# Turning the last product: w_down and W' as weights, h and o as the moving operand

## The chip, the cores and the metric

The kernel runs on one core of one Trainium2 chip. The metric is the device time of one execution in microseconds (us), the median of several runs. Engines: TensorE (PE, with its weight loads as PEld), VectorE (DVE), ScalarE (ACT), GpSimd (POOL) and SyncE (SP). SP computes nothing; its queue issues most of the DMAs, one after the other in program order.

## The reference

With S = 2048 tokens, D = 512, 32 heads of 16, F = 1792, all in float32:

```
g   = sigmoid((x * gate_w).sum(-1))                       one number per token
q, k, v = heads of x @ wqkv;  phi(t) = where(t > 0, t + 1, exp(t)) + 1e-6
kv  = sum_s phi(k)_s v_s^T;   z = sum_s phi(k)_s           per head
o   = phi(q) @ kv / (phi(q) . z + 1e-6)
h   = (x @ w_gate) * (x @ w_up)
out = g * (o @ wo) + (1 - g) * (h @ w_down)                [2048, 512]
```

## The kernel before

**Precision.** Every float32 operand of the large products is split into a high and a low part in a form that TensorE multiplies at full rate. `mm3` (it calls `mm`, line 52) makes each product of three matmuls: high by high, high by low, low by high. `split` (line 66) makes the parts: ACT copies the high one (`act`, line 58), DVE subtracts (`tt`, line 61). `stt` (line 64) is DVE's operation with a scalar and two tensors.

**Stage 1** (`p1`, to about 92 us). It goes through x in 16 tiles of 128 tokens, makes k, phi(k), the matrix G = phi(k)^T x (four PSUM banks `gt`), z, and on DVE the gate sum of every token as a column of `scol` [128, 16] (line 262). After the loop come the z store (`zpark`), and four small operations that turn `scol` into `gcol` = g and `ocol` = 1 - g, one column for each block of 128 tokens (lines 348 to 351).

**Stage 2** (`p2`, the rest). Two *pairs* of chunks of 512 tokens, and for each pair 16 *units*: 14 slices of 128 columns of w_gate and w_up (`f`) and two (`q`), after slices 5 and 9, of q. A unit (`unit`) computes a 2x2 block product with seven products instead of eight (Strassen's scheme in a form with sums of x blocks and of weight blocks), in four PSUM banks Y, X, R and S of one buffer each. Banks R and S are seeded by DVE (`bR<-bX,m`, `bS<-t,bX`) before PE accumulates on them, and DVE's `t<-bR,cross` reads R between PE's product 1 and product 6 into R. For an `f` unit the result is h for two chunks (`hh`, `hl`: [128 features, 2 chunks, 512 tokens]).

The order of the work is written out by hand: all operations of PE, ACT, DVE and SP's DMAs keep program order (`keep_in_program_order`). `later(n, place, fn)` puts work into unit n at a named place, `do(n, place)` runs it; the places of a unit come in the order high, low, e, m, c, d, t, s, r, end. `w_load(n+3)` follows unit n.

**The last product.** `wp_unit` folds kv and wo into W' (four row blocks, parked in DRAM), so that o @ wo becomes (phi(q) / den) @ W'. Two units' h with two row blocks of w_down (`dh`, `dl`, split by `down_weights` from the load `wdr`, first thing at place e), or o of a `q` unit with two row blocks of W', form a *group*. `down_jobs` makes a list of 8 jobs of it, one for every block of 128 tokens of the pair. A job is six matmuls of 512 columns into a PSUM bank `pdn` (tags dn and att, two buffers each), with the h or o slice as weights and w_down or W' moving; then the bank, scaled by g or 1 - g of its tokens (a column, one number per partition), is added to the block's accumulator `acc` [128 tokens, 512] in SBUF (ACT for the first group, else DVE, line 64). With the ninth group (`ends`) the block is complete and goes out: by POOL's queue for pair 0, by SP's for pair 1 (line 595). The very last job is cut into two halves of 256 columns. `share(n)` says how many jobs run at four points of unit n; what is left runs after the last unit.

**The denominators.** `attention` sends phi(q) z terms through DRAM, adds them (`z_add`, `z_end`), takes the reciprocal (`recip`, tile [128, 128]), stores it, and loads it back broadcast over the 16 columns of a head; `norm_high` multiplies phi(q) by it.

`bmask` is a [128, 128] mask for the heads that is last read in unit 2 (`kv_split`). Tag `cb` has three buffers of [128, 512], used to prepare x sums for pair 1 until unit 13.

Of the kernel before, what the change touches and what calls it, by code (L numbers as in the profile page):

```python
# [7 lines left out]
F32 = mybir.dt.float32  # L8
F32R = mybir.dt.float32r
AF = mybir.ActivationFunctionType  # L10
# [15 lines left out]
NPAIR = NC // 2  # L26
TPP = 2 * CH // P
EPS = 1e-6
WARM = 8
LEAD = 4  # L30
HB = 8
# [12 lines left out]
def gated_mix(ctx: ExitStack, tc, xt, xp, x, wqkv, wq, wq_add, wo, wgu, wgu_add, wdn, gate_w, out):  # L44
# [12 lines left out]
    def act(dst, src, func=AF.Copy, **kw):  # L57
        pin(nc.scalar.activation(dst, src, func, **kw))  # L58
# [4 lines left out]
    def stt(dst, a, scalar, b, op0, op1):  # L63
        pin(nc.vector.scalar_tensor_tensor(dst, a, scalar, b, op0=op0, op1=op1))  # L64
# [9 lines left out]
    def mm3(dst, lhs, rhs, start, stop, on=False, late=0, part=range(3)):  # L74

        (lh, ll), (rh, rl) = lhs, rhs
        three = ((lh, rh), (ll, rh), (lh, rl)) if late else ((lh, rh), (lh, rl), (ll, rh))
        for i in part:
            mm(dst, *three[i], start=start and i == 0, stop=stop and i == 2, skip_group_check=on)
# [9 lines left out]

    epsc = const.tile([P, 1], F32, name="epsc")  # L90
    scol = const.tile([P, 2 * NT + 8], F32, name="scol")[:, 0:NT]
    gcol = const.tile([P, NT], F32, name="gcol")
    ocol = const.tile([P, NT], F32, name="ocol")
    zcol = const.tile([P, KT], F32, name="zcol")
    ezcol = const.tile([P, KT], F32, name="ezcol")
    bmask = const.tile([P, P], F32, name="bmask")
# [20 lines left out]
    xpark = {i: [dram.tile([P, 2, CH], F32, name=f"xpark{i}{v}") for v in "hl"] for i in (2, 3, 4)}  # L117
    xsum = {i: dram.tile([P, 2, CH], F32, name=f"xsum{i}") for i in (1, 5, 6, 7)}

    zpark = dram.tile([KT * KT, P, P // KT], F32, name="zpark")  # L120
    wpark = [[dram.tile([P, D], F32, name=f"wpark{b}{v}") for v in "hl"] for b in range(KT)]

# [58 lines left out]
    with tc.tile_pool(name="p1", bufs=2, reuse_waits="tile") as p1:  # L181
# [163 lines left out]
        dma(zpark.rearrange("c l e -> l c e"), zacc.rearrange("l (c e) -> l c e", e=P // KT))  # L345


        act(gcol, scol, AF.Exp, scale=-1.0)
        pin(nc.vector.tensor_scalar_add(gcol, gcol, 1.0))
        pin(nc.vector.reciprocal(gcol, gcol))  # L350
        pin(nc.vector.tensor_scalar(ocol, gcol, -1.0, 1.0, op0=ALU.mult, op1=ALU.add))


    p2 = ctx.enter_context(tc.tile_pool(name="p2", bufs=1, reuse_waits="tile"))
# [203 lines left out]
            dma(there, part.bitcast(F32))  # L558


    acc = {}

    parts = [(1, 0), (0, 1), (1, 1), (0, 0)]
    banks = ["dn", "dn"]
    left = {(p, i): NF // 2 + 1 for p in range(NPAIR) for i in range(TPP)}

    def down_jobs(pair, group, col):

        def job(i):
            t = pair * TPP + i  # L570
            c, sl = divmod(i, CH // P)
            sl = slice(sl * P, (sl + 1) * P)
            s = col[:, t:t + 1]
            first = (pair, i) not in acc
            if first:
                acc[pair, i] = p2.tile([P, D], F32, tag="acc", name="acc", bufs=8)
            else:
                left[pair, i] -= 1
            ends = not left[pair, i]

            step = D // 2 if ends and pair and i == TPP // 2 - 1 else D
            for o in range(0, D, step):
                cols = slice(o, o + step)
                banks.reverse()
                pd = psum.tile([P, D], F32, tag=banks[0], name="pdn", bufs=2)[:, 0:step]
                for j, ((hh, hl), w2) in enumerate(group() if callable(group) else group):
                    mm3(pd, (hh[:, c, sl], hl[:, c, sl]), [v[:, cols] for v in w2], j == 0, j == 1)
                a = acc[pair, i][:, cols]
                if first:
                    act(a, pd, scale=s)  # L590
                else:
                    stt(a, pd, s, a, ALU.mult, ALU.add)
                if ends:
                    to = nc.gpsimd if pair == 0 else nc.sync
                    tc.keep_in_program_order(to.dma_start(out[t * P:(t + 1) * P, cols], a))

        return [lambda i=i: job((i + TPP // 2) % TPP) for i in range(TPP)]


    def attention(pair, j, n):  # L600
        phs, group, wrow = {}, {}, {}
        den = {}
        turns = n + 5 == units

        terms = dram.tile([KT, 4 * HB, DH, P], F32, name=f"terms{pair}{j}")
        there = dram.tile([4 * HB, KT, P], F32, name=f"den{pair}{j}")

        def quad(r, c, q):

            ex = p2.tile([P, CH], F32, tag="z", name="ex", bufs=4)  # L610
            act(ex, q, AF.Exp)
            ph = phs[r, c] = p2.tile([P, CH], F32, tag="ph", name="phq", bufs=4)
            act(ph, q, AF.Relu)
            stt(ph, ex, 1.0, ph, ALU.min, ALU.add)

        def z_part(i):
            r, c = parts[i]
            b = 2 * j + r
            z = p2.tile([P, CH], F32, tag="z", name="zq", bufs=4)
            act(z, phs[r, c], AF.Identity, scale=zcol[:, b:b + 1], bias=ezcol[:, b:b + 1])  # L620
            dma(terms[:, HB * i:HB * (i + 1)].rearrange("c h e t -> (h e) c t"), z.rearrange("p (c t) -> p c t", c=KT))

        def z_load(e):

            den[e] = p2.tile([P, KT, P], F32, tag="z", name="zt", bufs=4)
            dma(den[e], terms[:, :, e * KT:(e + 1) * KT].rearrange("c h e t -> (c h) e t"))

        def z_add(e):
            tt(den[0], den[0], den[e], ALU.add)

        def z_end():
            z = den[0]
            tt(z[:, 0:2], z[:, 0:2], z[:, 2:4], ALU.add)
            den["d"] = p2.tile([P, P], F32, tag="den", name="den")
            stt(den["d"], z[:, 0], EPS, z[:, 1], ALU.add, ALU.add)

        def recip():
            d = den["d"]
            pin(nc.vector.reciprocal(d, d))
            dma(there.rearrange("h c t -> c h t"), d)  # L640

        def norm(i):
            r, c = parts[i]
            if r not in group:
                group[r] = hidden()
            rb = p2.tile([P, CH], F32, tag="z", name="rb", bufs=4)
            one = there[HB * i:HB * (i + 1)].rearrange("h c t -> h (c t)")
            dma(rb, one[:, None, :].to_broadcast([HB, DH, CH]))
            den[i] = rb

        def norm_high(i):
            r, c = parts[i]
            stt(den[i], phs[r, c], EPS, den[i], ALU.add, ALU.mult)
            act(group[r][0][:, c], den[i])

        def norm_low(i):
            r, c = parts[i]
            hh, hl = group[r]
            tt(hl[:, c], den[i], hh[:, c].bitcast(F32), ALU.subtract)

        def weights():
            for r in range(2):
                wrow[r] = down_tiles()
                for src, part in zip(wpark[2 * j + r], wrow[r]):
                    dma(part.bitcast(F32), src)

        def last():

            where = len(jobs) if turns else 0
            jobs[where:where] = down_jobs(pair, lambda: [(group[r], wrow[r]) for r in range(2)], gcol)  # L670

        for i in range(4):
            later(n + 1, "e", lambda i=i: z_part(i))
        for e in range(4):
            later(n + 1, "t", lambda e=e: z_load(e))
        for e, place in zip((1, 2, 3), ("s", "s", "end")):
            later(n + 2, place, lambda e=e: z_add(e))
        later(n + 2, "end", z_end)
        later(n + 2, "end", recip)
        for i in range(4):  # L680
            later(n + 3, "e", lambda i=i: norm(i))
        for i, places in enumerate((((n + 3, "s"), (n + 3, "r")), ((n + 3, "end"), (n + 4, "e")),
                                    ((n + 4, "c"), (n + 4, "d")), ((n + 4, "t"), (n + 4, "s")))):
# [39 lines left out]
    for n, (i, k) in enumerate((i, k) for i in (2, 3, 4, 1, 6, 7) for k in range(2)):  # L723
        later(n, "s", lambda i=i, k=k: cb_load(i, k))
        later(n + 1, "c", lambda i=i, k=k: x_add(cb[i, k], 1, i, k))
        later(n + 2, "e", lambda i=i, k=k: cb_split(i, k))
    later(1, "r", lambda: dma(xsum[5], xp[1, SUMS[5][1]]))
    wdr = {}

    ffn = [n for n, u in enumerate(order) if u[1] == "f"]  # L730
# [11 lines left out]
    for n, (pair, kind, m) in enumerate(order):  # L742
        entry = {}
        if n == 6:

            banks[0] = "att"

        def down_weights(n=n, entry=entry):
            entry["d"] = down_tiles()
            split(*entry["d"], wdr.pop(n))  # L750
            d_load(ffn.index(n) + 2)

        if kind == "f":
            at.setdefault((n, "e"), []).insert(0, down_weights)
        hid = unit(n, attention(pair, m, n) if kind == "q" else None)
        w_load(n + 3)
        if kind == "f":
            if half is None:
                half = (hid, entry["d"])
            else:  # L760
                jobs += down_jobs(pair, (half, (hid, entry["d"])), ocol)
                half = None
        do(n, "end")
    down(2)
# [55 lines left out]
```

## Time and profile before

| what | us |
|---|---|
| three runs | 603.41, 603.61 (median), 603.97 |
| span of the profiled execution, first to last instruction | 601.4 |
| PE busy in the span | 596.5 |
| DVE busy | 441.9 |
| ACT busy | 309.2 |

No time is listed for the profiled execution beside its span. Of the span, the first 5 us are loads and a warm-up of TensorE, and the last 3.5 us come behind the last matmul. A busy PE means that matmuls overlap without a pause: each has a duration of 389 ns in the profile, but the next starts after 227 ns. The DMA's share of busy time is about 60%. A row of a timeline reads: start in us from the span's start, duration, engine, line of the kernel, operation, out<-in by the program's tile names, shapes, how many in a row, and in brackets the idle time before it with what ended it.

### The profile page before, as it was taken

The page shows a single profiled execution, that of the slowest core. Times are in us where ns is not written, and L with a number is a line of the kernel's source. Part 1 is how long each engine was busy: PE and PEld are TensorE (multiplying, and loading weights), DVE is VectorE, ACT ScalarE, POOL GpSimd, SP SyncE. Part 2 cuts the span into 40 slices and gives each one's busy share as a digit, 9 for nine tenths or more (in the row PEclk, how much of TensorE's full clock was granted, in tenths as well). Part 3 has the DMA queues.
Part 4 walks back from the last instruction along what each step waited for, and adds up shares of the span by engine and source line. Part 5 has one row for each costly group of instructions (what it writes and reads, how often), then busy time and mean ns, then how long its engine had stood idle before and what let it go on. Part 6 is the DMA issues. An engine that isn't in the chain of part 4 may idle for free.

```text
span 601.4 us, 7610 instructions
## 1 busy us (share of the span) xinstructions
PE 596.5 (99%) x2682; PEld 492.1 (82%) x2682; DVE 441.9 (73%) x693; ACT 309.2 (51%) x534; POOL 47.1 (8%) x63
## 2 busy tenths in 40 slices
PE   9999999999999999999999999999999999999997
PEld 6888888888888888888888888888888888888886
DVE  6977896776787689666888866456677986668864
ACT  3855765586449545373444534654474454643300
POOL 0011100000111110100000020010000000000000
PEclk9999999999999999999999999999999999999999
DMA  8577948667868969658479535334386563553303
GB/s 291 182 195 136 288 94 276 153 189 193 219 175 203 275 156 269 135 126 209 105 223 350 155 138 134 89 87 90 70 192 171 150 168 67 130 146 81 102 1 141
DMA packets 51046, 98.54 MB, mean 164 GB/s; under 512 B 6576, under 2 KB 17584, under 8 KB 50992
## 3 DMA queue, kind: packets, MB, share of 16 engines
q1 hardware_dynamic: 43312, 69.22, 34.1%
q0 software_dynamic: 7408, 28.32, 26.1%
q10 hardware_dynamic: 288, 0.52, 0.3%
q8 instruction: 21, 0.34, 0.2%
q14 instruction: 17, 0.14, 0.1%
HBM read 82.31 MB, written 16.25 MB: 164 GB/s over the span
## 4 chain that ended last, share of the span: by engine, by line
PE 99%; DVE 0%; issue 0%
PE pdn L52 33%; PE bR L52 15%; PE bY L52 14%; PE bX L52 14%; PE pk L52 7%; PE bS L52 7%; PE gt L52 7%; PE warm L52 1%; PE pw L52 0%; PE pkv L52 0%; DVE acc L64 0%; DVE xc1h L108 0%
## 5 line engine op out<-in xcount | busy, mean ns | idle before, releaser
L52 PE MATMUL pdn<-dl,hh 128*128 128x512 f32 x290 | 112.4, 388 | 0.0
L52 PE MATMUL pdn<-dh,hl 128*128 128x512 f32 x290 | 112.4, 388 | 0.0
L52 PE MATMUL pdn<-dh,hh 128*128 128x512 f32 x290 | 112.4, 388 | 0.0
L64 DVE SCALAR_TENSOR_TENSOR acc<-pdn,ocol,acc 128x512 f32<-128x512 f32 (+1 forms) x97 | 71.2, 742 | 30.2 <-PE pdn L52 30.0
L58 ACT ACTIVATE hh<-cross 128x512 fp32r<-128x512 f32 x56 | 35.2, 628 | 89.6 <-DVE cross L61 89.6
L61 DVE TENSOR_TENSOR wcl<-wr,wch 128x512 fp32r<-128x512 f32 (+1 forms) x96 | 73.2, 771 | 0.0
L52 PEld LDWEIGHTS pdn<-dh,hh 128*128 128x128 f32 x290 | 54.5, 188 | 11.2
L52 PEld LDWEIGHTS pdn<-dl,hh 128*128 128x128 f32 x290 | 54.5, 188 | 11.2
L52 PEld LDWEIGHTS pdn<-dh,hl 128*128 128x128 f32 x290 | 54.5, 188 | 11.1
L58 ACT ACTIVATE wch<-wr 128x512 fp32r<-128x512 f32 (+1 forms) x96 | 60.1, 694 | 0.0
L52 PE MATMUL bX<-xbh,wch 128*128 128x512 f32 x128 | 49.8, 389 | 0.0
L52 PE MATMUL bX<-xbl,wch 128*128 128x512 f32 x128 | 49.8, 389 | 0.0
L52 PE MATMUL bX<-xbh,wcl 128*128 128x512 f32 x128 | 49.8, 389 | 0.0
L61 DVE TENSOR_TENSOR bR<-bX,m 128x512 f32<-128x512 f32 x32 | 22.3, 696 | 36.6 <-PE bX L52 31.7
L85 POOL DMA_DIRECT2D wr<-in_wgu_add x28 | 24.3, 868 | 309.5 <-ACT wr L58 175.2
L58 ACT ACTIVATE cross<-bY 128x512 f32<-128x512 f32 x32 | 19.1, 598 | 50.6 <-PE bY L52 50.2
L61 DVE TENSOR_TENSOR t<-bR,cross 128x512 f32<-128x512 f32 x32 | 22.1, 690 | 24.9 <-PE bR L52 11.5
L61 DVE TENSOR_TENSOR hl<-cross,hh 128x512 fp32r<-128x512 f32 x56 | 38.2, 683 | 0.8
L58 ACT ACTIVATE wr<-wr 128x512 f32<-128x512 f32 x64 | 36.5, 620 | 1.2 <-DMA wr<-in_wgu 1.2
L64 DVE SCALAR_TENSOR_TENSOR acc<-pdn,gcol,acc 128x512 f32<-128x512 f32 x32 | 23.7, 749 | 17.5 <-PE pdn L52 17.4
L58 ACT ACTIVATE cross<-bX 128x512 f32<-128x512 f32 x32 | 19.1, 597 | 32.8 <-DVE bS L61 32.6
L58 ACT ACTIVATE m<-bY 128x512 f32<-128x512 f32 x32 | 19.1, 597 | 22.4 <-PE bY L52 22.2
(158 smaller groups left out, 1256.6 us busy)
## 6 DMA issues: line engine op xcount, KB each, us to landing
wr<-in_wgu_add POOLq DMA_DIRECT2D x28, 640.0 KB, 6.3
wr<-in_wgu SPq DMA_DIRECT2D x28, 384.0 KB
wdr<-in_wdn SPq DMA_DIRECT2D x28, 256.0 KB
xraw<-in_x SPq DMA_DIRECT2D x16, 256.0 KB
terms<-zq SPq DMA_DIRECT2D x16, 256.0 KB
zt<-terms SPq DMA_DIRECT2D x16, 256.0 KB
rb<-den SPq DMA_DIRECT2D x16, 256.0 KB
xtraw<-in_xt SPq DMA_DIRECT2D x12, 256.0 KB
```

The lines of the kernel that those rows point to most:

```text
L52: tc.keep_in_program_order(nc.tensor.matmul(*args, **kw))
L58: pin(nc.scalar.activation(dst, src, func, **kw))
L61: pin(nc.vector.tensor_tensor(dst, a, b, op=op))
L64: pin(nc.vector.scalar_tensor_tensor(dst, a, scalar, b, op0=op0, op1=op1))
L85: tc.keep_in_program_order(nc.gpsimd.dma_start(dst, src, accum_op=ALU.add))
```

## The change

The last product changes sides. A job now takes one chunk of 512 tokens (c) and one block of 128 output features (d): slices of w_down or W' are the weights, h or o of the whole chunk moves, and the accumulator holds [128 features, 512 tokens]. The output is stored as [512, 2048] (and turned on the host).

Since tokens now lie along the free dimension, the gate of a token is no number per partition any more. The sums use out = (1 - g) * (r * a + b) with r = g / (1 - g) = exp(s), s limited to 40:

- r goes into the reciprocals of the denominators: `recip` multiplies them by a table of r [128, 128], loaded into `bmask` once per pair (`ratio_load`).
- 1 - g is multiplied onto finished accumulators: each completing job runs one more DVE operation by a row `og` that is broadcast to all partitions (`gate_load`, two tiles of tag `cb` per pair).
- To get there, `gates` [128, 32] (r and 1 - g) is turned by DVE in blocks of 32x32 into `turned`, and four DMAs on SP's queue store it in DRAM (`grow`); they stand in program order behind the `zpark` store and ahead of the first loads of stage 2. At the end of unit 2 eight small DMAs from DRAM to DRAM spread r into `rtab`.

```diff
-    gcol = const.tile([P, NT], F32, name="gcol")
-    ocol = const.tile([P, NT], F32, name="ocol")
+    gates = const.tile([P, 2 * NT], F32, name="gates")
...
+    grow = dram.tile([2, NT, P], F32, name="grow")
+    rtab = dram.tile([NPAIR, KT, 4, HB, P], F32, name="rtab")
...
-        act(gcol, scol, AF.Exp, scale=-1.0)
-        pin(nc.vector.tensor_scalar_add(gcol, gcol, 1.0))
-        pin(nc.vector.reciprocal(gcol, gcol))
-        pin(nc.vector.tensor_scalar(ocol, gcol, -1.0, 1.0, op0=ALU.mult, op1=ALU.add))
+        ratio, rest = gates[:, 0:NT], gates[:, NT:2 * NT]
+        pin(nc.vector.tensor_scalar(scol, scol, GMAX, None, op0=ALU.min))
+        act(ratio, scol, AF.Exp)
+        pin(nc.vector.tensor_scalar_add(rest, ratio, 1.0))
+        pin(nc.vector.reciprocal(rest, rest))
+        turned = p1.tile([P, 2 * NT], F32, name="turned", bufs=1)
+        pin(nc.vector.transpose(turned, gates))
+        step = 2 * NT
+        for q in range(P // step):
+            dma(grow.rearrange("v t p -> (v t) p")[:, q * step:(q + 1) * step], turned[q * step:(q + 1) * step])
...
-    acc = {}
+    acc, og = {}, {}
...
-    def down_jobs(pair, group, col):
+    def gate_load(pair):
+        for c in range(2):
+            og[pair, c] = p2.tile([P, CH], F32, tag="cb", name="og", bufs=3)
+            t = (pair * 2 + c) * (CH // P)
+            dma(og[pair, c], grow[1, t:t + CH // P].rearrange("t p -> (t p)")[None, :].to_broadcast([P, CH]))
+
+    def ratio_load(pair):
+        dma(bmask, rtab[pair].rearrange("c i h t -> (c i h) t"))
+
+    def down_jobs(pair, group):
...
-            c, sl = divmod(i, CH // P)
-            sl = slice(sl * P, (sl + 1) * P)
-            s = col[:, t:t + 1]
+            c, d = divmod(i, KT)
+            sl = slice(d * P, (d + 1) * P)
...
-            step = D // 2 if ends and pair and i == TPP // 2 - 1 else D
-            for o in range(0, D, step):
+            step = CH // 2 if ends and pair and i == TPP // 2 - 1 else CH
+            for o in range(0, CH, step):
...
-                    mm3(pd, (hh[:, c, sl], hl[:, c, sl]), [v[:, cols] for v in w2], j == 0, j == 1)
+                    mm3(pd, [v[:, sl] for v in w2], (hh[:, c, cols], hl[:, c, cols]), j == 0, j == 1, late=1)
...
                 if first:
-                    act(a, pd, scale=s)
+                    act(a, pd)
                 else:
-                    stt(a, pd, s, a, ALU.mult, ALU.add)
+                    tt(a, pd, a, ALU.add)
                 if ends:
+                    tt(a, a, og[pair, c][:, cols], ALU.mult)
                     to = nc.gpsimd if pair == 0 else nc.sync
-                    tc.keep_in_program_order(to.dma_start(out[t * P:(t + 1) * P, cols], a))
+                    t = (pair * 2 + c) * CH
+                    tc.keep_in_program_order(to.dma_start(out[sl, t + o:t + o + step], a))
...
             pin(nc.vector.reciprocal(d, d))
+            tt(d, d, bmask, ALU.mult)
             dma(there.rearrange("h c t -> c h t"), d)
...
+    def ratio_rows():
+        for pair in range(NPAIR):
+            for i, (_, c) in enumerate(parts):
+                t = (pair * 2 + c) * KT
+                dma(rtab[pair][:, i], grow[0, t:t + KT][:, None, :].to_broadcast([KT, HB, P]))
+
+    later(2, "end", ratio_rows)
+    for pair in range(NPAIR):
+        later(pair * units + 6, "r", lambda pair=pair: ratio_load(pair))
+        later(pair * units + 14, "r", lambda pair=pair: gate_load(pair))
...
-    args.append(nc.dram_tensor("out_0", (S, D), F32, kind="ExternalOutput").ap())
+    args.append(nc.dram_tensor("out_0", (D, S), F32, kind="ExternalOutput").ap())
```

More of the change, by code (lines that the diff above doesn't have):

```diff
@@ L28 @@
 EPS = 1e-6
+GMAX = 40.0
 WARM = 8
@@ L565, in gated_mix @@
     left = {(p, i): NF // 2 + 1 for p in range(NPAIR) for i in range(TPP)}
-    def down_jobs(pair, group, col):
+    def gate_load(pair):
[6 more added lines that the diff above has]
+    def down_jobs(pair, group):
         def job(i):
-            t = pair * TPP + i
-            c, sl = divmod(i, CH // P)
-            sl = slice(sl * P, (sl + 1) * P)
-            s = col[:, t:t + 1]
+            c, d = divmod(i, KT)
+            sl = slice(d * P, (d + 1) * P)
             first = (pair, i) not in acc
             if first:
-                acc[pair, i] = p2.tile([P, D], F32, tag="acc", name="acc", bufs=8)
+                acc[pair, i] = p2.tile([P, CH], F32, tag="acc", name="acc", bufs=8)
             else:
@@ L579, in job @@
             ends = not left[pair, i]
-            step = D // 2 if ends and pair and i == TPP // 2 - 1 else D
-            for o in range(0, D, step):
+            step = CH // 2 if ends and pair and i == TPP // 2 - 1 else CH
+            for o in range(0, CH, step):
                 cols = slice(o, o + step)
                 banks.reverse()
-                pd = psum.tile([P, D], F32, tag=banks[0], name="pdn", bufs=2)[:, 0:step]
+                pd = psum.tile([P, CH], F32, tag=banks[0], name="pdn", bufs=2)[:, 0:step]
                 for j, ((hh, hl), w2) in enumerate(group() if callable(group) else group):
-                    mm3(pd, (hh[:, c, sl], hl[:, c, sl]), [v[:, cols] for v in w2], j == 0, j == 1)
+                    mm3(pd, [v[:, sl] for v in w2], (hh[:, c, cols], hl[:, c, cols]), j == 0, j == 1, late=1)
                 a = acc[pair, i][:, cols]
                 if first:
-                    act(a, pd, scale=s)
+                    act(a, pd)
                 else:
-                    stt(a, pd, s, a, ALU.mult, ALU.add)
+                    tt(a, pd, a, ALU.add)
                 if ends:
+                    tt(a, a, og[pair, c][:, cols], ALU.mult)
                     to = nc.gpsimd if pair == 0 else nc.sync
-                    tc.keep_in_program_order(to.dma_start(out[t * P:(t + 1) * P, cols], a))
+                    t = (pair * 2 + c) * CH
+                    tc.keep_in_program_order(to.dma_start(out[sl, t + o:t + o + step], a))
         return [lambda i=i: job((i + TPP // 2) % TPP) for i in range(TPP)]
@@ L669, in last @@
             where = len(jobs) if turns else 0
-            jobs[where:where] = down_jobs(pair, lambda: [(group[r], wrow[r]) for r in range(2)], gcol)
+            jobs[where:where] = down_jobs(pair, lambda: [(group[r], wrow[r]) for r in range(2)])
         for i in range(4):
@@ L760, in gated_mix @@
             else:
-                jobs += down_jobs(pair, (half, (hid, entry["d"])), ocol)
+                jobs += down_jobs(pair, (half, (hid, entry["d"])))
                 half = None
@@ L818 @@
     r = run_bass_kernel_spmd(nc, [arrays], core_ids=[0])
-    return r.results[0]["out_0"].reshape(1, S, D)
+    return np.ascontiguousarray(r.results[0]["out_0"].T).reshape(1, S, D)
```

## The prediction, on record before the result

> **What bounds the kernel now.** I read the page's busy times first, then the table by stretch, then the chain of waits in order of time, and last the timelines of VectorE (DVE), ScalarE (ACT) and SyncE (SP, whose queue issues most DMAs) at the places that the diff touches.
>
> ```profile
> span 601.4 us, 7610 instructions
> ...
> PE 596.5 (99%) x2682; PEld 492.1 (82%) x2682; DVE 441.9 (73%) x693; ACT 309.2 (51%) x534; POOL 47.1 (8%) x63
> ```
>
> The table by stretch, cut at the first real product, around the change of pairs, and at the last product:
>
> ```profile
> 4.96:597.87 592.91, 592.91 (x2674) 491.01 (x2674) 440.25 (x688) 307.26 (x532) 45.99 (x56) 1.00 0.61 164
> 325.60:366.40 40.80, 40.80 (x181) 33.80 (x181) 30.19 (x42) 16.34 (x27) 6.18 (x10) 1.00 0.60 174
> 597.87:601.37 3.50, 0.00 (x0) 0.00 (x0) 0.48 (x1) 0.00 (x0) 0.00 (x0) 1.00 0.41 150
> ```
>
> TensorE (PE) is busy for all 592.91 us between its first real product and its last, at a granted clock of 1.00. So there is nothing to win by removing a wait inside: the time falls only if PE gets fewer or shorter matmuls, and it rises by whatever is put behind the last matmul (now 3.50 us), or wherever PE is made to wait. The profile's span is 601.4 and the median of the runs 603.61, so 2.2 us lie outside the span; I leave them alone and add my changes to the median.
>
> **PE's own work.** The number of matmuls stays: before, 8 token blocks x 512 features, now 2 chunks x 4 feature blocks x 512 tokens, six matmuls for each job; the last job is cut into two halves both times. Only the roles change. In the chain, six matmuls whose weight is a w slice (bank Y, where x moves) stand next to six whose weight is h (pdn):
>
> ```profile
> 116.35 1.36 PE bY L52 x6
> 117.71 1.36 PE pdn L52 x6
> ```
>
> Both take 1.36 us, 227 ns for each matmul. The trace thus has both roles, at one price: 0 us.
>
> **The tail.** A job that completes an output tile did one operation on DVE (scaled add); now it does an add and a multiply by the 1-g row, and its DMA waits for the second. This is DVE at the end, and SP's DMAs:
>
> ```profile
> 595.12 0.75 DVE L64 SCALAR_TENSOR_TENSOR acc<-pdn,ocol,acc 128x512 f32<-128x512 f32 x1 [0.61 <-PE pdn L52]
> 596.48 1.20 DVE L64 SCALAR_TENSOR_TENSOR acc<-pdn,ocol,acc 128x512 f32<-128x512 f32 x2 [0.61 <-PE pdn L52]
> 597.91 0.48 DVE L64 SCALAR_TENSOR_TENSOR acc<-pdn,ocol,acc 128x256 f32<-128x256 f32 x1 [0.23 <-PE pdn L52]
> ```
> ```profile
> 597.26 1.50 SPq L595 DMA_DIRECT2D out<-acc  x3
> ```
>
> Prices come from three places on DVE. The first is an add of PSUM and SBUF, 0.69 us; the second shows operations that do not need each other (0.60 from start to start, and 0.68 for one with both inputs in SBUF, hl); in the third one operation reads what the one before it wrote.
>
> ```profile
> 97.88 0.69 DVE L61 TENSOR_TENSOR t<-bR,cross 128x512 f32<-128x512 f32 x1 [0.21 <-ACT wr L58]
> ```
> ```profile
> 345.92 1.40 DVE L64 SCALAR_TENSOR_TENSOR acc<-pdn,gcol,acc 128x512 f32<-128x512 f32 x2
> 347.24 0.95 DVE L61 TENSOR_TENSOR wcl<-wr,wch 128x768 fp32r<-128x768 f32 x1
> 348.10 0.68 DVE L61 TENSOR_TENSOR cross<-bR,cross 128x512 f32<-128x512 f32 x1
> 348.96 0.69 DVE L61 TENSOR_TENSOR cross<-bS,cross 128x512 f32<-128x512 f32 x1 [0.17 <-PE bS L52]
> 349.56 0.68 DVE L61 TENSOR_TENSOR hl<-cross,hh 128x512 fp32r<-128x512 f32 x1
> 351.75 0.70 DVE L61 TENSOR_TENSOR bR<-bX,m 128x512 f32<-128x512 f32 x1 [1.50 <-PE bX L52]
> 352.35 0.68 DVE L61 TENSOR_TENSOR hl<-cross,hh 128x512 fp32r<-128x512 f32 x1
> ```
> ```profile
> 217.07 0.43 DVE L61 TENSOR_TENSOR zt<-zt 128x256 f32<-128x256 f32 x1
> 217.53 0.29 DVE L64 SCALAR_TENSOR_TENSOR den<-zt 128x128 f32<-128x128 f32 x1
> ```
>
> So a half costs 0.43, and a dependent operation starts 0.03 after the end of the first, where an independent one starts 0.08 before it. A full pair of add and multiply takes 0.69 + 0.03 + 0.60 = 1.32 us until the next add, just under the 1.36 us that PE needs for a job (595.12 to 596.48): no backlog builds up before the last job. Then: add of the last whole tile 596.48, its multiply 597.20, add of the first half 597.80, multiply 598.26, add of the second half 598.61, multiply 599.07, end 599.50. Before, the end was 597.91 + 0.48 = 598.39, and the DMA followed it at once (597.26 + 1.50 - one issue). **Tail: +1.1 us.** The lower bound is the last half alone, without the operations before it: 0.43 + 0.03 + 0.43 against 0.48, +0.4.
>
> The Trainium skill (VectorE: DVE Perf Modes, "The DRAIN you can't avoid") says that after each DVE operation the next one cannot start until the pipe is empty, and that chaining changes nothing. The trace does not agree: 0.60 from start to start where the duration is 0.69. By that rule a pair would take 1.38, a little over PE's 1.36, and my estimate of the tail would be +1.3.
>
> **The gates, and SP behind them.** This is the place where the change adds a wait. `turned` is stored by four DMAs that stand in SP's queue in program order: behind the zpark store and ahead of the first w_down load (wdr), the four wv and four wo loads. SP now stands until DVE has turned the gates. SP and DVE there:
>
> ```profile
> 87.55 0.38 SPq L82 DMA_DIRECT2D zpark<-zacc  x1
> 87.98 0.91 SPq L82 DMA_DIRECT2D wdr<-in_wdn  x1
> 88.95 2.31 SPq L82 DMA_DIRECT2D wv<-in_wqkv  x4
> 91.78 1.75 SPq L82 DMA_DIRECT2D wo_sb<-in_wo  x4
> ```
> ```profile
> 89.79 0.09 DVE L262 DVE_READ_ACCUMULATOR junk<-xraw,gw 128x1 f32 x1
> 90.16 0.17 DVE L349 TENSOR_SCALAR gcol<-gcol 128x16 f32<-128x16 f32 x1 [0.28 <-ACT gcol L58]
> 90.36 0.25 DVE L350 RECIPROCAL gcol<-gcol 128x16 f32<-128x16 f32 x1
> 90.65 0.17 DVE L351 TENSOR_SCALAR ocol<-gcol 128x16 f32<-128x16 f32 x1
> 90.74 0.68 DVE L503 COPY gts<-gt 128x512 f32<-128x512 f32 x1
> ```
> ```profile
> 166.92 0.21 DVE L541 STREAM_TRANSPOSE zrow<-zrow 128x32 f32<-128x32 f32 x1
> ```
>
> The gate sums are there at 89.88. Then come min 0.17 + 0.03, exponential on ACT 0.28 (the idle time in the 90.16 row), add 0.17 + 0.03, reciprocal 0.25 + 0.03, transpose 0.21 by the zrow row: about 91.1. Four DMAs at the spacing of the wo loads (1.75 / 4 = 0.44) bring wdr to 92.85 instead of 87.98, 4.9 us later. (DVE's gts copy slips by 0.3, into the idle time before its next operation; the product that needs it stands a whole unit later.) Who waits for wdr is ACT in unit 0, and behind it on ACT, in order, three wch copies and the copy of bank Y that DVE's `t` needs; PE may write bank R again only when `t` has read it:
>
> ```profile
> 94.24 0.62 ACT L58 ACTIVATE dh<-wdr 128x512 fp32r<-128x512 f32 x1
> 94.76 1.88 ACT L58 ACTIVATE wch<-wr 128x512 fp32r<-128x512 f32 x3
> 96.54 0.58 ACT L58 ACTIVATE cross<-bY 128x512 f32<-128x512 f32 x1
> ```
> ```profile
> 98.98 0.39 PE L52 MATMUL bR<-xc6h,wch 128*128 128x512 f32 x1
> ```
>
> How long a 256 KB load takes on SP from issue to landing has no row. The nearest are the same size on POOL's queue, and the last store above: issued at about 598.4, with all of the program's end done at 601.4, so under 3.0.
>
> ```profile
> out<-acc POOLq DMA_DIRECT2D x8, 256.0 KB, 3.2
> ```
>
> I take 2.8, nearer to the one on the same queue. wdr lands at 95.65, dh starts 1.45 late; 2.30 us after dh's start (96.54 - 94.24) comes the bank-Y copy, at 98.0, done 98.57; `t` runs 98.6 to 99.3; PE's next product into R, so far at 98.98, starts at 99.35. **Stall in unit 0: +0.4 us**, which PE never gets back. Landing after 2.4 us or less makes it 0; 3.2 makes it 0.8, and a slower issue (0.58 each, as the wv loads with their waits) another 0.5: 0 to 1.3.
>
> The Trainium skill (DMA: Bandwidth & Descriptors, "Anatomy of one DMA") gives about 2.0 us fixed and 436 GB/s, measured on the other kind of queue. That makes an estimate of 2.6 us for 256 KB, and a stall of 0.2; the POOL row's 3.2 us is longer than that.
>
> **What I cost at nothing.** The eight small `rtab` DMAs after unit 2 meet an idle SP queue:
>
> ```profile
> 128.00 0.33 SPq L82 DMA_DIRECT2D wr<-in_wgu  x1
> 131.97 0.33 SPq L82 DMA_DIRECT2D wdr<-in_wdn  x1
> ```
>
> At 0.44 to 0.58 each they need 3.5 to 4.6 us, and 3.6 are free; the wdr load behind them slips by 1 us at most, and its user is in the next unit. Ratio and gate loads are three DMAs a pair, a unit or more ahead of their use; if one were late, the multiply would hold DVE, and PE only after four PSUM buffers. The multiply behind the four reciprocals (0.29 + 0.03) delays DVE's seed of bank R, but PE first runs product 4 (1.36) and a job. Scaled adds become plain ones (0.75 to 0.69): DVE was not the limit. At the change of pairs two completing jobs come at 345.92 and six in the next unit: two multiplies put 2 x 0.60 us ahead of the cross products, and the 1.50 us idle before bR at 351.75 takes that up; the other six are spread over a unit.
>
> **The rivals.**
> 1. *Cover holds*: wdr lands in time and only the tail is left, 603.61 + 1.1 = 604.7. For it: the stall hangs on 0.4 us of an unseen latency. This is not slower by what can be told apart: 0.2% is 1.2 us, about what a measurement of this kernel can tell from no change.
> 2. *DVE becomes the bound at the change of pairs.* DVE is busy 30.19 of 40.80 us there; eight multiplies add 8 x 0.60 = 4.8. If they fall ahead of seeds of R and S rather than into idle time, or if wdr lands so late that several products of unit 0 wait, PE loses another 1 to 2 us: about 606.6. Against it: the 1.50 us of slack just quoted.
> 3. *Faster*: moving h instead of loading it as a weight shortens PE's spacing. 870 matmuls of this product would have to gain over 3 ns each of their 227 to pay for 1.1 + 0.4 and 1.2 more; at 5 ns it is 870 x 0.005 = 4.4 us, 600.7. Against it stand the two 1.36 rows.
>
> **How the numbers follow.** Tail and a stall in unit 0, 603.61 + 1.1 + 0.4 = 605.1: chance 0.56. Rival 1 has 0.23, rival 2 has 0.17, rival 3 has 0.04. The range goes from the tail with a shorter chain (604.4) to rival 2 (606.8). Slower by over 0.2%: 0.56 + 0.17 = 0.73; within 0.2%: 0.23; faster: 0.04.
>
> **What would show it.** Right: pdn still 1.36 us for six; DVE's last multiply ends about 1.1 us after PE's end moved by the same shift; SP shows four `grow` stores from about 91.1 and wdr near 92.9; ACT shows idle time before dh<-wdr, and PE a gap of some tenths before bR near 99. Wrong: wdr issued before 91, no gap on PE in unit 0, gaps on PE between 345 and 370, or another spacing of pdn.

## The result and the profile after

The changed kernel takes 605.20 us (median of 7 runs, 605.07 to 606.09), the kernel before 603.63 (7 runs, 603.12 to 603.97). The medians lie 1.57 us apart. The ratio over all runs is 1.0031, with a 95% interval of 1.0021 to 1.0042: slower by 1.3 to 2.5 us. The forecast was 605.1.

The page of the changed kernel, its first line and the busy times, and then the row of the table by stretch that goes from the first real product to the last:

```profile
span 604.2 us, 7655 instructions
...
PE 597.8 (99%) x2682; PEld 492.7 (82%) x2682; DVE 447.1 (74%) x715; ACT 308.1 (51%) x534; POOL 47.1 (8%) x63
```
```profile
4.96:599.42 594.46, 594.18 (x2674) 491.63 (x2674) 444.21 (x707) 306.21 (x532) 45.97 (x56) 1.00 0.62 166
```

TensorE (PE) still runs the same 2682 matmuls, but the stretch is 1.55 us longer (594.46 against 592.91), and 0.28 us of it are idle. The span is 2.8 us longer than the one of before, more than the medians differ. The next views show why.

**Unit 0.** The timelines of SP, ACT, DVE and PE of the changed kernel (start, duration, engine, line, operation):

```profile
88.50 0.38 SPq L83 DMA_DIRECT2D zpark<-zacc  x1
92.05 1.73 SPq L83 DMA_DIRECT2D grow<-turned  x4
93.89 0.36 SPq L83 DMA_DIRECT2D wdr<-in_wdn  x1
```
```profile
96.69 0.63 ACT L59 ACTIVATE dh<-wdr 128x512 fp32r<-128x512 f32 x1 [1.41 <-DMA wdr<-in_wdn]
97.23 1.88 ACT L59 ACTIVATE wch<-wr 128x512 fp32r<-128x512 f32 x3
99.01 0.58 ACT L59 ACTIVATE cross<-bY 128x512 f32<-128x512 f32 x1
```
```profile
99.62 0.69 DVE L62 TENSOR_TENSOR t<-bR,cross 128x512 f32<-128x512 f32 x1 [0.37 <-ACT cross L59]
```
```profile
99.70 0.39 PE L53 MATMUL bX<-xbh,wcl 128*128 128x512 f32 x1
100.37 0.50 PE L53 MATMUL bR<-xc6h,wch 128*128 128x512 f32 x1 [0.28 <-DVE t L62]
100.71 0.40 PE L53 MATMUL bR<-xc6l,wch 128*128 128x512 f32 x1
```

SP stands from 88.9 to 92.05, until the gates are turned. The first w_down load, second in SP's queue before, leaves at 93.89. ACT waits 1.41 us for it; the copy of bank Y, `t` and product 6 follow. From 99.70 PE's next start comes after 0.67 us instead of 0.23, and the one after that takes 0.34: 0.55 us lost, 0.44 of it the wait and 0.11 a slow restart.

**The tail.** DVE's last six operations:

```profile
598.09 0.69 DVE L62 TENSOR_TENSOR acc<-pdn,acc 128x512 f32<-128x512 f32 x1
598.81 0.69 DVE L62 TENSOR_TENSOR acc<-acc,og 128x512 f32<-128x512 f32 x1
599.42 0.42 DVE L62 TENSOR_TENSOR acc<-pdn,acc 128x256 f32<-128x256 f32 x1
599.88 0.43 DVE L62 TENSOR_TENSOR acc<-acc,og 128x256 f32<-128x256 f32 x1
600.22 0.42 DVE L62 TENSOR_TENSOR acc<-pdn,acc 128x256 f32<-128x256 f32 x1
600.67 0.42 DVE L62 TENSOR_TENSOR acc<-acc,og 128x256 f32<-128x256 f32 x1
```

From the add of the last whole tile to DVE's end it is 3.00 us (598.09 to 601.09); before, 1.91 (596.48 to 598.39). That is +1.09. From DVE's end to the end of the span it is 3.1 against 3.0.

**The start.** The last part of the longer span lies ahead of all work that the change touches. These are the first products, six matmuls to the row that is quoted last, in the profile of before and in that of the changed kernel:

```profile
4.96 0.70 PE L52 MATMUL pk<-wkh,xah 128*128 128x512 f32 x2
...
6.46 0.63 PE L52 MATMUL pk<-wkh,xah 128*128 128x512 f32 x2
```
```profile
4.96 1.20 PE L53 MATMUL pk<-wkh,xah 128*128 128x512 f32 x2
...
7.43 0.63 PE L53 MATMUL pk<-wkh,xah 128*128 128x512 f32 x2
```

The same six matmuls take 1.50 us in one and 2.47 in the other: 0.97 us. So the span's 2.8 us are 0.97 at the start, 0.55 in unit 0, 1.09 on DVE at the end, 0.1 behind it, and 0.1 in small pieces. Whether the start belongs to the change is a question for the runs below.

### The profile page after: what moved, and what is told of

Same layout as the page of the kernel before. It is cut to its first block, busy times and chain, and to the rows that moved or that the text cites. A ratio compares the mean times of both kernels' runs of the same rounds, so it can differ in the third digit from the quotient of the medians.

```text
span 604.2 us, 7655 instructions
## 1 busy us (share of the span) xinstructions
PE 597.8 (99%) x2682; PEld 492.7 (82%) x2682; DVE 447.1 (74%) x715; ACT 308.1 (51%) x534; POOL 47.1 (8%) x63
## 4 chain that ended last, share of the span: by engine, by line
PE 95%; DVE 3%; ACT 1%; DMA 0%; SPq 0%; issue 0%; ACTq 0%
PE pdn L53 31%; PE bR L53 14%; PE bY L53 14%; PE bX L53 14%; PE pk L53 7%; PE bS L53 7%; PE gt L53 6%; DVE acc L62 2%; PE warm L53 1%; DMA wdr<-in_wdn 0%; PE pw L53 0%; PE pkv L53 0%; ACT wch L59 0%; SPq L83 0%; DVE xbl L62 0%
## 5 line engine op out<-in xcount | busy, mean ns | idle before, releaser
L62 DVE TENSOR_TENSOR acc<-pdn,acc 128x512 f32<-128x512 f32 x129 | 87.5, 684 | 44.1 <-PE pdn L53 43.4
L53 PE MATMUL pdn<-hh,dl 128*128 128x512 f32 x290 | 112.4, 388 | 0.0
L53 PE MATMUL pdn<-hh,dh 128*128 128x512 f32 x290 | 112.4, 388 | 0.0
L53 PE MATMUL pdn<-hl,dh 128*128 128x512 f32 x290 | 112.4, 388 | 0.0
L53 PEld LDWEIGHTS pdn<-hh,dh 128*128 128x128 f32 x290 | 54.4, 188 | 11.3
L53 PEld LDWEIGHTS pdn<-hh,dl 128*128 128x128 f32 x290 | 54.4, 188 | 11.1
L53 PEld LDWEIGHTS pdn<-hl,dh 128*128 128x128 f32 x290 | 54.4, 188 | 11.1
L53 PEld LDWEIGHTS bX<-xbh,wch 128*128 128x128 f32 x128 | 24.0, 188 | 5.0
```

Source lines behind the costliest of these rows:

```text
L53: tc.keep_in_program_order(nc.tensor.matmul(*args, **kw))
L62: pin(nc.vector.tensor_tensor(dst, a, b, op=op))
```

## The experiments

Times are medians of 5 to 12 runs; each is compared with the kernel before on the same chip (603.2 to 603.6). Without another word an edit is made to the changed kernel. In the edits that move the stores, `turned` lies in spare columns of the `scol` tile.

### Is it the late w_down load? (store_late, eight_stores, wdr_first)

store_late puts the gate stores behind the first loads:

```diff
     d_load(0)
     wp_load()
     d_load(1)
+    gate_store()
```

> The four gate stores go out behind the first w_down, wv and wo loads instead of ahead of them; nothing else changes. Theory (two places: a stall in unit 0 behind the late w_down load, and a longer tail): the w_down load is issued near 88 us again, ACT does not wait for it, the gap on TensorE before product 6 of unit 0 (666 + 341 ns against 227 each in the changed kernel, so 0.55 us) is gone, and the time falls by 0.5 us to about 604.7. Rival (the added time sits in the first products at half pitch, which the changed kernel's profile shows, or in VectorE's load at the change of pairs): the gap may go, but the time stays at 605.2.

604.58 us, 1.0020 (1.0011 to 1.0028) of before. SP issues the w_down load at 87.92 again, and PE goes through unit 0 without a gap:

```profile
98.69 0.39 PE L53 MATMUL bX<-xbh,wcl 128*128 128x512 f32 x1
98.92 0.39 PE L53 MATMUL bR<-xc6h,wch 128*128 128x512 f32 x1
```

It is 0.6 us faster than the changed kernel (0.5 was forecast), and none of its 11 runs is slower than the fastest of the changed kernel's 7. eight_stores goes the other way:

```diff
-        for q in range(P // step):
+        for q in 2 * list(range(P // step)):
```

> The four gate stores are issued twice, so that the first w_down load stands behind eight. Theory: 4 more at 0.43 us put the load 1.75 us later, ACT's wait in unit 0 grows from 1.4 to about 3.1 us, and since the slack is used up already, TensorE's gap before product 6 grows by the same 1.75 us: about 606.9. Rival (the unit-0 gap is a small constant, not tied to the load): 605.2 to 605.5.

607.09 us, 1.0072 (1.0056 to 1.0089). SP, then PE:

```profile
91.12 3.94 SPq L83 DMA_DIRECT2D grow<-turned  x8
95.12 0.41 SPq L83 DMA_DIRECT2D wdr<-in_wdn  x1
```
```profile
98.78 0.39 PE L53 MATMUL bX<-xbh,wcl 128*128 128x512 f32 x1
101.57 0.50 PE L53 MATMUL bR<-xc6h,wch 128*128 128x512 f32 x1 [2.40 <-DVE t L62]
```

Four more stores take 2.2 us on SP (3.94 - 1.73), and PE's gap grows from 0.67 to 2.79, by 2.1. The load's lateness passes one to one to PE, since the slack is used up. The time grows by 1.9, but it is no clean measure of that gap: in this profile the first six products take 1.5 us instead of 2.5, and PE loses another 0.5 us at 236, behind a wait of DVE for the load of the denominators:

```profile
229.96 0.69 DVE L65 SCALAR_TENSOR_TENSOR rb<-phq,rb 128x512 f32<-128x512 f32 x1 [0.69 <-DMA rb<-den]
```

This wait is in 4 of the 12 profiles of the changed kernel and its variants (0.26 to 0.69 us on DVE, 0.1 to 0.5 lost on PE, store_late among them with 0.32 and 0.2), and in neither of the two of the kernel before. The multiply by r puts the store of the denominators 0.33 us further behind the reciprocal's start (0.98 us before, 1.31 in the changed kernel); that this is the cause was not tested. wdr_first asks whether that one load is all:

```diff
     d_load(0)
+    gate_store()
     wp_load()
     d_load(1)
```

> Only the first w_down load is put ahead of the four gate stores; the wv and wo loads stay behind them, 3 us later than in the kernel before. Theory: what PE waits for in unit 0 is that one load, through ACT's queue: the gap before product 6 of unit 0 is gone as in store_late, time as store_late (604.6). Rival (the other loads matter as well, or the stores themselves slow the loads): a gap remains in units 0 or 1 and the time stays near 605.2.

605.20 us, 1.0031 (1.0021 to 1.0041), runs from 604.50 to 607.01. The time agrees with the rival, the trace with the theory: no gap is left in unit 0,

```profile
99.24 0.39 PE L53 MATMUL bX<-xbh,wcl 128*128 128x512 f32 x1
99.47 0.39 PE L53 MATMUL bR<-xc6h,wch 128*128 128x512 f32 x1
```

nor is there another one anywhere but at the start. So the late wv and wo loads cost PE nothing in this profile (the table under before_again has the whole stretch). The timed runs do not confirm the 0.6 us here; the first six products took 2.0 us in the profile, and what they took in the other runs is not known.

### Is it the multiply in the tail? (no_last_mult, late_no_mult, only_last_mult, tiles_on_pool)

no_last_mult leaves the multiply out for pair 1:

```diff
-                    tt(a, a, og[pair, c][:, cols], ALU.mult)
+                    if pair == 0:
+                        tt(a, a, og[pair, c][:, cols], ALU.mult)
```

> The multiply by 1-g on finished tiles is left out for pair 1 (so the second half of the output lacks that factor). Theory: VectorE's last operation ends 1.1 us earlier relative to TensorE's last product, and the time falls by 1.1 us to about 604.1; what is left over before is the unit-0 stall of about 0.5. Rival (start or change of pairs): the multiply is hidden or small, 605.0 to 605.2.

604.30 us, 1.0015 (1.0006 to 1.0023): 0.9 less than the changed kernel. DVE ends as early after the last whole tile as before:

```profile
597.65 1.14 DVE L62 TENSOR_TENSOR acc<-pdn,acc 128x512 f32<-128x512 f32 x2 [0.67 <-PE pdn L53]
599.08 0.42 DVE L62 TENSOR_TENSOR acc<-pdn,acc 128x256 f32<-128x256 f32 x1 [0.29 <-PE pdn L53]
```

597.65 to 599.50 is 1.85, against 3.00 with the multiplies. late_no_mult makes both edits.

> Both: stores behind the loads, and no multiply by 1-g on the finished tiles of pair 1 (left out of the result). Theory: the two costs add, and nothing else of the change costs time: 605.2 - 0.5 - 1.1 = 603.6, the time of the kernel before. Rival: at least half a microsecond stays above it, 604.2 or more, from the new loads, the turned roles or pair 0's multiplies.

604.09 us, 1.0015 (1.0007 to 1.0024). That is 1.1 less than the changed kernel, not 1.6, and 0.67 above before, where the forecast was nothing. In its profile, no gap on PE and no longer tail is left except at the start, where the first six matmuls take 2.3 us; before_again below deals with that. Taken by itself, the edit of the stores gains only 0.2 us here (604.30 to 604.09); the gap that it removes was 0.34 us in the profile of no_last_mult.

only_last_mult keeps the multiply of the last job's halves and leaves out those of the seven tiles before:

```diff
+                    if pair == 0 or i == TPP // 2 - 1:
```

> As the changed kernel, but of pair 1's finished tiles only the last job's two halves are multiplied by 1-g; the seven tiles before lack the factor in the output. GpSimd does nothing here. Theory (two parts of the longer tail: 0.65 from the multiply of the job before the last, ahead of the halves in VectorE's queue, and 0.45 from the last half's own multiply): VectorE's end comes 1.3 us after the last matmul's start (1.89 with all multiplies, 0.74 with none, 0.80 before), the time is 0.6 below the changed kernel, 604.6. Rival (only the last half's own operations count): 1.89 still.

604.65 us, 1.0016 (1.0004 to 1.0028), 0.55 less than the changed kernel:

```profile
597.21 1.14 DVE L62 TENSOR_TENSOR acc<-pdn,acc 128x512 f32<-128x512 f32 x2 [0.67 <-PE pdn L53]
598.38 0.42 DVE L62 TENSOR_TENSOR acc<-acc,og 128x256 f32<-128x256 f32 x1
598.73 0.42 DVE L62 TENSOR_TENSOR acc<-pdn,acc 128x256 f32<-128x256 f32 x1
599.18 0.42 DVE L62 TENSOR_TENSOR acc<-acc,og 128x256 f32<-128x256 f32 x1
```

597.21 to 599.60 is 2.39. So of the 1.09 us in the tail, 0.6 come from the multiply of the tile before the last job, which stands ahead of the halves on DVE (3.00 - 2.39), and the rest from the halves' own. tiles_on_pool tried to win those 0.6 with the computation complete:

```diff
+                    if pair and i != TPP // 2 - 1:
+                        pin(nc.gpsimd.tensor_tensor(a, a, og[pair, c][:, cols], op=ALU.mult))
+                    else:
                         tt(a, a, og[pair, c][:, cols], ALU.mult)
```

> The changed kernel with pair 1's multiplies of finished tiles on GpSimd, all but the two halves of the last job, which stay on VectorE. Theory (0.6 to 0.7 us of the longer tail come from the multiply of the job before the last, which stands ahead of the halves on VectorE, 0.45 from the last half's own multiply): VectorE's end comes 1.3 us after the last matmul's start instead of 1.89 (before: 0.80), the time falls by 0.6 to 604.6; the unit-0 gap stays. Rival (the tail is set by the last half and its store alone): 1.89 and 605.2 as before.

605.35 us, 1.0032 (1.0021 to 1.0044): nothing won. DVE's first half-multiply takes 1.15 us instead of 0.43, while GpSimd works until 596.88 + 2.63 = 599.51. The two adds of PSUM and SBUF ahead of it, also beside GpSimd's work, take 1.14 as in no_last_mult:

```profile
597.47 1.14 DVE L62 TENSOR_TENSOR acc<-pdn,acc 128x512 f32<-128x512 f32 x2 [0.67 <-PE pdn L53]
598.64 1.15 DVE L62 TENSOR_TENSOR acc<-acc,og 128x256 f32<-128x256 f32 x1
```
```profile
596.88 2.63 POOL L610 TENSOR_TENSOR acc<-acc,og 128x512 f32<-128x512 f32 x2
```

DVE's multiply ends 0.28 after GpSimd's, as if it had stood still for most of that time. The expectation missed this. The Trainium skill has it (SBUF — State Buffer, "SBUF: two separate sides"): DVE with two inputs in SBUF and GpSimd share a pair of ports, and whichever comes second waits for the other's whole instruction. The trace agrees in that 0.72 us; a multiply that begins only at 599.51 would end 0.43 later and not 0.28, but GpSimd's times are rough.

### Is it DVE at the change of pairs? (no_mult_pair0)

```diff
+                    if pair:
```

> The multiply by 1-g is left out for pair 0's finished tiles (their half of the output lacks the factor); pair 1 keeps it. Theory: those eight multiplies lie beside PE's work, so the time stays that of the changed kernel, 605.2, within 0.3, and PE shows no other gap. Rival (VectorE is the bound at the change of pairs): the time falls by 0.5 to 2 us.

605.47 us, 1.0041 (1.0026 to 1.0057), its fastest run 605.02 beside 605.07 of the changed kernel. Nothing is won, and in its profile PE takes the same 587.67 us as in the changed kernel from its 25th product to its last (table below). So the eight multiplies of pair 0 lie beside PE's work.

### Is it the start? (before_again)

The kernel before once more, measured against itself.

> The kernel before, measured against itself: how far two medians of one program lie apart, and how its first products run in a second profile. One account (the half-pitch start of the products in the changed kernel's profile is chance, and differs from execution to execution in every kernel): the ratio's interval holds 1, the two medians differ by up to 0.3 us, and the second profile may show the first six products taking anything from 1.5 to 2.5 us. Rival (the slow start belongs to the changed kernel): again 1.5 us, and late_no_mult's remainder of 0.67 us over the kernel before is a cost of the change that is not found yet.

603.22 us against 603.19, ratio 0.9995 (0.9986 to 1.0004). Its second profile:

```profile
4.95 1.20 PE L52 MATMUL pk<-wkh,xah 128*128 128x512 f32 x2
...
7.00 0.61 PE L52 MATMUL pk<-wkh,xah 128*128 128x512 f32 x2
```

The same six matmuls take 2.05 us here and 1.50 in the first profile of the same program. So the start varies from execution to execution of one program. In the 12 profiles of the changed kernel and its variants these six take 1.5 to 2.7 us. A measure without them goes from the start of PE's 25th product, where the spacing is 0.23 us in every profile, to the start of its last:

| profile | first six, us | 25th product to last, us | last matmul's start to DVE's end, us |
|---|---|---|---|
| before | 1.5 | 587.01 | 0.80 |
| before_again | 2.0 | 587.03 | 0.80 |
| changed | 2.5 | 587.67 | 1.89 |
| no_mult_pair0 | 2.7 | 587.67 | 1.89 |
| store_late | 1.5 | 587.19 | 1.89 |
| wdr_first | 2.0 | 587.02 | 1.89 |
| no_last_mult | 2.3 | 587.37 | 0.74 |
| late_no_mult | 2.3 | 587.03 | 0.74 |

Two profiles of the kernel before agree within 0.02 us by this measure, and late_no_mult and wdr_first agree with them: with the first w_down load ahead of the stores, PE loses nothing more to the change. (store_late's 0.2 is the wait for the denominators.) So the two costs are shown in the traces. What late_no_mult still has above before is accounted for by its one profile (0.8 at the start, 0.1 each for a later first product and the last store) but not shown by timed runs. The two medians of one program lay 0.03 apart here, which speaks against chance alone for 0.67 us; whether the changed kernels start slowly more often is open.

### A version without both costs? (h_scaled, factor_on_pool, h_scaled_quarters)

With r a + b and a factor 1-g on everything, the factor can be put on the sum before the last group and on h of the last group, so that the last job is a plain add. h_scaled does so for pair 1, with the stores late:

```diff
+                if left[pair, i] == (1 if pair else 0):
+                    tt(a, a, og[pair, c][:, cols], ALU.mult)
...
             tt(cross[:, 1], bank["R"], cross[:, 1], ALU.mult)
+            if n >= len(order) - 2:
+                tt(cross[:, 1], cross[:, 1], og[1, 1], ALU.mult)
```

(the same for chunk 0, and the gate rows of pair 1 are loaded two units earlier).

> Complete computation. Stores behind the loads, and for pair 1 the factor 1-g moves off the tail: it is multiplied onto the accumulators one group earlier and onto the h of the last two units (four more multiplies of 128x512 on VectorE, in units 30 and 31), so that the last job is a plain add again. Theory: unit-0 gap gone, VectorE's last operation 0.75 us after the last matmul's start (1.89 in the changed kernel), PE without new gaps: the time of the kernel before, 603.4 to 603.7. Rival (VectorE becomes late in the last units, since every multiply costs 0.6 of its time): a gap on PE in units 30 to 31 or in the last jobs, 604.2 or more.

604.48 us, 1.0017 (1.0008 to 1.0025): the rival's time. The tail is short again, but in unit 30 ACT and PE show

```profile
563.68 0.63 ACT L59 ACTIVATE hh<-rb 128x512 fp32r<-128x512 f32 x1 [2.50 <-DVE rb L65]
564.22 0.58 ACT L59 ACTIVATE m<-bY 128x512 f32<-128x512 f32 x1
```
```profile
564.85 0.50 PE L53 MATMUL bY<-xc4h,wch 128*128 128x512 f32 x1 [0.91 <-ACT m L59]
```

Two more multiplies on DVE delay `rb`; ACT waits for it, the copy of bank Y stands behind on ACT, and PE waits for that bank: starts 1.29 and 0.34 us apart instead of 0.23, 1.2 us lost. factor_on_pool moves those multiplies to GpSimd, onto the copies of banks Y and X:

```diff
         act(cross[:, 1], bank["X"])
+        if n >= len(order) - 2:
+            pin(nc.gpsimd.tensor_tensor(cross[:, 1], cross[:, 1], og[1, 1], op=ALU.mult))
```

> As h_scaled (complete computation, stores behind the loads, no multiply in the tail), but the four multiplies on the way to h of units 30 and 31 run on GpSimd, on the copies of banks Y and X that the products are multiplied with, so that they are not in VectorE's queue. Theory (what cost h_scaled its gain was 1.3 us more on VectorE ahead of rb, for which ACT and behind it the copy of bank Y waited, a PE gap of 1295 + 337 ns): the gap is gone, everything else as h_scaled, so the time of the kernel before within 0.3, 603.4 to 603.8. Rival (GpSimd is too slow for its place: a multiply of 128x512 takes over 3 us between the copy of X and its use, or slows VectorE): a gap in units 30 or 31, 604.2 or more.

604.12 us, 1.0014 (1.0002 to 1.0026), from 603.36 to 605.92. A smaller gap stays at the same place (0.43 and 0.34 apart, 0.3 us lost). GpSimd and DVE ahead of it, and PE:

```profile
556.22 1.29 POOL L446 TENSOR_TENSOR cross<-cross,og 128x512 f32<-128x512 f32 x1 [0.27 <-ACT cross L59]
556.78 1.28 DVE L62 TENSOR_TENSOR wcl<-wr,wch 128x512 fp32r<-128x512 f32 x1
```
```profile
563.91 0.39 PE L53 MATMUL pdn<-hl,dh 128*128 128x512 f32 x1
564.34 0.50 PE L53 MATMUL bY<-xc4h,wch 128*128 128x512 f32 x1
```

DVE's subtraction `wcl`, with two inputs in SBUF, takes 1.28 us here instead of 0.68: 0.6 us longer beside GpSimd's multiply, as in tiles_on_pool. The `rb` behind it on DVE and ACT's work behind that come later by as much, and by the order of the queues this is what PE's gap is made of; no run takes it apart. The trace is thus the rival's (GpSimd slows VectorE), and the time lies a little under the rival's 604.2. It is the fastest complete version with turned roles, about 1 us below the changed kernel, and does not beat the kernel before. h_scaled_quarters cuts the last job of h_scaled into four:

```diff
-            step = CH // 2 if ends and pair and i == TPP // 2 - 1 else CH
+            step = CH // 4 if ends and pair and i == TPP // 2 - 1 else CH
```

> As h_scaled, with the last job cut into four pieces of 128 columns instead of two of 256. Theory (the end is one VectorE operation and one store behind the last matmul): VectorE's last add falls from 0.42 to about 0.29 us, 0.1 us less than h_scaled. Rival: 24 short matmuls take longer than 12, or four stores queue on SP at 0.38 us each: 0.1 to 0.5 us more than h_scaled.

606.02 us, 1.0041 (1.0029 to 1.0053), the rival, and by more than it said: 1.5 us over h_scaled. In the profiles 0.9 of that is a slower start (2.5 us for the first six against 1.6). A matmul of 128 columns starts every 0.11 us, little less than the 0.12 of one of 256:

```profile
598.55 0.28 PE L53 MATMUL pdn<-hh,dl 128*128 128x128 f32 x1
598.67 0.27 PE L53 MATMUL pdn<-hl,dh 128*128 128x128 f32 x1
```

So 24 of them take about 2.7 us where 12 of 256 take 1.4.

## Why the prediction was right, point by point

**PE's own work: right.** Both roles still cost the same in the chain of the changed kernel:

```profile
117.90 1.36 PE bY L53 x6
119.26 1.36 PE pdn L53 x6
```

Over the whole kernel the table above says the same: 587.03 us in late_no_mult, 587.01 before.

**The tail: right.** +1.1 was forecast, +1.09 is in the trace, with the pieces in the order that was worked out (dependent 0.03 apart; an independent add 0.61 after the multiply's start, 598.81 to 599.42). Two experiments take it apart into 0.6 and 0.5. The rule of the Trainium skill (VectorE: DVE Perf Modes, "The DRAIN you can't avoid") that each operation waits for an empty pipe, +1.3, does not fit; the section adds that an operation which is not held starts earlier, and that is what the trace shows. Not priced: 0.1 us between DVE's end and the end of the span; that this is the wider stride of the stored rows was not tried.

**The gates and SP: right.** From the gate sums (90.81) to the first store (92.05) it was 1.24 us, forecast 1.2; four stores and the step to the load took 1.84, forecast 1.75; from the load's issue to ACT's start it was 2.80 us (93.89 to 96.69), the value taken; ACT waited 1.41, forecast 1.45. The stall was 0.55 instead of 0.4: the wait itself was 0.44, and after it PE's second matmul came 0.34 us later instead of 0.23, a cost that the sum had left out. In the profiles of the four other kernels with the same four stores ahead of the load the stall is 0.34 to 0.63, so that a forecast of 0.4 could not be closer than that. The estimate by the Trainium skill (DMA: Bandwidth & Descriptors, "Anatomy of one DMA"), 2.6 us for the load, was 0.2 below what was measured. That the load alone makes the gap is shown (eight_stores, wdr_first). The 0.6 us in the time are shown by store_late, not by wdr_first.

**Costs taken as nothing: nearly right in the sum, two wrong in size.** The `rtab` DMAs took 6.5 us on SP, not 3.5 to 4.6, and the w_down load behind them went out some 3 us later, not 1:

```profile
129.77 6.50 SPq L83 DMA_DIRECT2D rtab<-grow  x8
136.38 0.39 SPq L83 DMA_DIRECT2D wdr<-in_wdn  x1
```

The user of that load is in the next unit, and PE has no gap there. Of the multiply behind the reciprocals the prediction followed only the delay of bank R's seed, not that of the denominators' own store and loads; the wait for them (eight_stores above) cost PE nothing in the changed kernel's profile and 0.1 to 0.5 us in four others. At the change of pairs the idle time before bR shrank from 1.50 to 0.28 us, by the 1.2 that two multiplies were said to take, and no gap came of it:

```profile
353.36 0.70 DVE L62 TENSOR_TENSOR bR<-bX,m 128x512 f32<-128x512 f32 x1 [0.28 <-ACT hh L59]
```

**The rivals.** (The price of rival 2 stands as 606.6 in its item and as 606.8 in the range.) *Cover holds* fell with the gap in unit 0, *DVE becomes the bound* with no_mult_pair0 (h_scaled shows that another place has less room: two such multiplies in unit 30 made PE lose 1.2 us), *faster* with the two 1.36 rows.

The sum of 1.5 us meets the 1.57 of the medians. The parts in the trace make 1.74 (0.55 + 1.09 + 0.1), and the start can add or take half a microsecond and more. The two places and their sizes were right for the reasons given; that the sum meets the medians to 0.1 us is luck.

## What to carry to other kernels

When the bottleneck engine has no gap, an edit to other engines cannot shorten the stretch in which it is busy: look for what is put behind its last operation, and for what is put ahead of something in an in-order queue. A few small DMAs that wait for a late result belong behind the loads of the next stage, not ahead of them, even if nobody needs them soon. A factor that was nearly free inside a scaled add (0.75 us against 0.69) becomes an operation of its own when its index moves to the free dimension, and it costs time where no matmul hides it: in the last job, and in the tile just before it. When runs of one program start differently, compare the traces from a point behind the start.

## What the runs showed of the hardware that was not expected

- The first real products start at 0.43 us spacing in some executions and at 0.23 in others, of one program: 1.50 and 2.05 us for the first six in two profiles of the kernel before, and 2.47 in the changed one, with a granted clock of 1.00 in all of these profiles, also in the stretch from 4.9 to 7.5 us. The Trainium skill (TensorE: Matmul & The Clock Gate, Part 1) says that TensorE begins at half rate and is released by an activity window that does not start with the kernel, so that the point varies. The spacing, 0.43 against 0.23, and its varying end agree; the granted clock does not show it. That makes it a likely account and not a shown one.
- GpSimd's multiply made DVE's multiply of two SBUF tensors 0.72 us longer (tiles_on_pool), and a subtraction of two SBUF tensors 0.60 longer (factor_on_pool), while two adds of PSUM and SBUF beside it kept their 1.14. Where DVE's subtraction started first (factor_on_pool, at 554.12, GpSimd at 554.29), it kept its 0.68, and GpSimd's multiply took 1.67 instead of 1.29.
- After a wait, PE's second matmul started 0.34 us after the first instead of 0.23, in every gap of 0.4 us or more that these profiles show.
